# Attention with normalized queries and keys, then a spatially gated MLP: the first sixth of a hand-written instruction order laid out anew, and the last stores on two queues

## The chip, the cores and the metric

The kernel runs on one core of a Trainium2 chip. The metric is the device time of one execution, in microseconds (us). A core has a matrix engine (TensorE, PE in the profile), three other compute engines (ScalarE, ACT; VectorE, DVE; GpSimd, POOL), a synchronization engine that here only issues transfers (SyncE, SP), and 16 DMA engines that all queues share. Each engine works through its own instructions in program order; semaphores order work between engines.

## The reference

Eight batches of 12 heads, 448 positions, head size 64. The result of the attention, heads side by side (768 wide), is the input of a gated MLP.

```python
q_n, k_n = (rmsnorm(q, g_q), rmsnorm(k, g_k))      # x / sqrt(mean(x*x) + 1e-6) * g
scores = scale * np.matmul(q_n, k_n.transpose(0, 1, 3, 2))
attn = np.exp(scores - max); attn = attn / (sum(attn) + 1e-09)
x = heads side by side of np.matmul(attn, v)        # (8, 448, 768)
h = np.maximum(x @ w_in, 0.0);  u, v = two halves of h  # 512 each
v_n = (v - mean(v)) / np.sqrt(var(v) + 1e-06)
v_s = np.einsum('ts,bsd->btd', w_spatial, v_n) + b_spatial[None, :, None]
out = (u * v_s) @ w_out                             # (8, 448, 768), float32
```

## The kernel before

The 96 heads are worked in 24 groups of four, three groups to a batch. A group's q or k is a tile `raw` of 128 partitions x 896 (four heads, seven columns of 64 positions). Group 0 is loaded and normalized in two halves, so that the pipeline starts sooner. Queries and keys of the first four groups are turned by TensorE; those of later groups by transposing DMAs on SyncE's queue. The kernel leaves out the maximum before the exponential and divides at the end by sums that TensorE makes against a tile of ones.

All instructions are issued in one order, written out by hand or by a planner as the string `PLAN`; the kernel's last loop reads it word by word. A word `name.args/slots/engine` calls `op_name`; slots are buffer or PSUM bank numbers, the engine is a (ScalarE), v (VectorE), g (GpSimd) or s (SyncE). An engine thus gets its instructions in the order of the words that fall to it, and a word moved ahead or behind others on the same engine moves in that engine's queue. Buffers are reused, and an instruction also waits until its target's last reader is through: ten `raw` tiles, three of squares, 22 of exponentials, eight PSUM banks. VectorE and GpSimd operations between SBUF tiles (norms, squares) are made to take turns in the order of the plan.

The words that the text needs, with the line of the profile:

| word | what it does | engine, line |
| --- | --- | --- |
| `l.i.r`, `L.G.i` | load half r of group 0, or all of group G; i = 0 is q, 1 is k | SyncE, L309, L296 |
| `q`, `Q` / `r`, `R` | squares / their sums per row | a, v or g, L392, L394 / v, L411, L405 |
| `i`, `I` / `j`, `J` | Ln, then Exp: one over the root of the mean square | a, L428, L418 / L431, L423 |
| `n`, `N` | normalize | v or g, L446, L438 |
| `p`, `P` / `k`, `K` | transposes on TensorE / their eviction, keys times the gains | PE, L465, L457 / a or v, L373, L375, L476 |
| `T`, `Z` | transposing DMA / gains onto the turned keys | SyncE, L493 / a or v, L474, L476 |
| `S.G.u`, `E.G.u` | scores of one of the seven units of a group / their exponential | PE, L518 / a, L526 |
| `s`, `a`, `b` | one of seven passes that add up the sums, the first and the second half of attention times values | PE, L551 |
| `D`, `d`, `X` | Ln and Exp of the sums (one over the sum) / the product into the MLP's input `xt` | a, L570, L574 / v, L580 |
| `v.b.n` | load values of batch b, with a change of type | POOL's software queue, L326 |
| `wi`, `ws`, `wo` | load pieces of `w_in`, the spatial weights, `w_out`, with a change of type | POOL's software queue, L333, L337, L340 |
| `wb`, `wx` | load and copy the spatial bias | SyncE, L344 / a or v |
| `gl`, `gA`, `gB`, `gC` | load the two gains (0.5 KB each), multiply them, turn them into a column | L305, L379, L384, L387 |
| `Y.m`, `y.m` | turn the spatial weights / evict them | PE, L360 / a or v, L373, L375 |
| `V`, `U`, `W` / `c`, `u` | products with `w_in`, and the tail rows / their evictions | PE, L596, L662, L625 / a or v, L587, L589 |
| `H`, `G`, `O`, `o`, `t` | spatial product, gating, output product, eviction, store | PE L676, v L681, PE L690, a or v L373, L375, SyncE L711, L714 |
| `z.n` | n matmuls of 64 columns of the identity that nothing reads | PE, L261 |

In the plan before, 140 of these `z` matmuls stand ahead of group 0's first transposes. ScalarE's order is q.1.0, q.0.0, q.0.1, i.0, j.0, q.1.1, Q.1.1, Q.1.0, i.1, j.1, I.1, J.1 and then the first exponential, E.0.1. The spatial weights are the third transfer that GpSimd issues, and their transposes stand among the first scores.

Of the kernel before, what the change touches and what calls it, by code (L numbers as in the profile page):

```python
# [756 lines left out]
```

## Time and profile before

| | |
| --- | --- |
| runs shown | 278.58 us median (276.86 to 279.51, three runs) |
| profiled execution | 277.75 us, its span 276.0 us |
| mean granted TensorE clock | 0.979 |
| TensorE busy | 257.9 us |
| ScalarE, VectorE, GpSimd busy | 218.0, 203.2, 144.9 us |
| moved by DMA | 51.14 MB |
| first exponential starts | 16.39 us |
| last matmul ends, last store lands | 270.6 us, 274.8 us |

The profile is of one execution; times in it count from the start of the span. "Busy" is the time in which an engine had an instruction under way, and for TensorE the ends are modelled. The granted clock is the share of full speed that TensorE was given. In a line of the timeline stand start, duration, engine, line of the kernel, operation, output and input tile, and in brackets the idle time before it with what ended it. DMA shares are a mean over 16 engines and can lie a little above 1.

### The profile page before, as it was taken

The page shows a single profiled execution, that of the slowest core. Times are in us where ns is not written, and L with a number is a line of the kernel's source. Part 1 is how long each engine was busy: PE and PEld are TensorE (multiplying, and loading weights), DVE is VectorE, ACT ScalarE, POOL GpSimd, SP SyncE. Part 2 cuts the span into 40 slices and gives each one's busy share as a digit, 9 for nine tenths or more (in the row PEclk, how much of TensorE's full clock was granted, in tenths as well). Part 3 has the DMA queues.
Part 4 walks back from the last instruction along what each step waited for, and adds up shares of the span by engine and source line. Part 5 has one row for each costly group of instructions (what it writes and reads, how often), then busy time and mean ns, then how long its engine had stood idle before and what let it go on. Part 6 is the DMA issues. An engine that isn't in the chain of part 4 may idle for free.

```text
span 276.0 us, 10147 instructions
## 1 busy us (share of the span) xinstructions
PE 257.9 (93%) x4372; PEld 136.0 (49%) x4389; DVE 203.2 (74%) x355; ACT 218.0 (79%) x357; POOL 144.9 (52%) x122
## 2 busy tenths in 40 slices
PE   7479999999999999999999999999998999999992
PEld 7365555365445445444454444444553545455550
DVE  3678999888869988987985588956976184748730
ACT  3388999999989999988998989988898865330632
POOL 3073895697746798957885669654990000000000
PEclk9859999999999999999999999999999999999998
DMA  7999997999979999899799999974589400114586
GB/s 207 291 330 279 258 198 90 255 233 231 201 146 167 364 206 179 185 285 173 223 192 246 273 251 246 172 97 69 71 126 215 142 2 2 30 29 114 128 296 208
DMA packets 63073, 51.14 MB, mean 185 GB/s; under 512 B 39602, under 2 KB 58675, under 8 KB 63027
## 3 DMA queue, kind: packets, MB, share of 16 engines
q1 hardware_dynamic: 54770, 42.22, 64.2%
q0 software_dynamic: 8256, 8.27, 19.6%
q8 instruction: 34, 0.56, 0.9%
q14 instruction: 13, 0.10, 0.1%
HBM read 38.55 MB, written 11.01 MB: 180 GB/s over the span
## 4 chain that ended last, share of the span: by engine, by line
PE 31%; DMA 9%; POOL 8%; issue 4%; ACT 3%; SPq 1%; DVE 0%; ACTq 0%; POOLq 0%
PE ps L690 6%; DMA vt<-in_v_dram 6%; PE ps L676 6%; PE ps L551 6%; PE ps L596 5%; PE ps L662 4%; POOL nrm L438 4%; PE ps L518 3%; POOL sqt L394 3%; DMA qT<-nrm 3%; ACT et L526 2%; PE ps L625 2%; POOL vt L326 1%; SPq L493 1%; ACT rc L574 0%
## 5 line engine op out<-in xcount | busy, mean ns | idle before, releaser
L526 ACT ACTIVATE et<-ps 128x896 bf16<-128x896 f32 x168 | 146.0, 923 | 12.7 <-PE ps L518 11.3
L438 POOL TENSOR_TENSOR nrm<-raw,rs 128x896 bf16<-128x896 f32 x40 | 67.3, 1691 | 27.6 <-ACT rs L423 9.6
L518 PE MATMUL ps<-qT,kT 64*32 64x448 bf16 x1344 | 61.7, 358 | 3.4 <-DVE kT L476 1.1
L394 POOL TENSOR_TENSOR sqt<-raw 128x896 f32<-128x896 f32 x28 | 46.8, 1680 | 16.9 <-DVE vn L653 9.2
L551 PE MATMUL ps<-et,vt 64*32 64x448 bf16 x1344 | 52.1, 350 | 2.0 <-DMA vt<-in_v_dram 1.0
L405 DVE TENSOR_REDUCE ss<-sqt 128x14 f32<-128x896 f32 x46 | 48.4, 1075 | 4.4 <-ACT sqt L392 3.1
L662 PE MATMUL ps<-xt,w_in 128*128 128x448 bf16 x192 | 43.4, 353 | 0.2
L518 PEld LDWEIGHTS <-kT 64*32 64x32 bf16 x1344 | 22.1, 90 | 32.4 <-issue 22.5
L580 DVE TENSOR_TENSOR xt<-ps,rc 128x448 bf16<-128x448 f32 x48 | 27.9, 617 | 12.0 <-ACT rc L574 6.9
L690 PE MATMUL ps<-w_out,gt 128*128 128x384 bf16 x192 | 36.5, 326 | 0.0
L596 PE MATMUL ps<-w_in,xt 128*128 128x512 bf16 x127 | 33.9, 380 | 0.9 <-issue 0.3
L551 PEld LDWEIGHTS <-vt 64*32 64x32 bf16 x1344 | 24.6, 92 | 16.2 <-issue 3.8
L373 ACT ACTIVATE os<-ps 128x384 f32<-128x384 f32 (+1 forms) x34 | 16.4, 491 | 15.1 <-PE ps L690 14.1
L676 PE MATMUL ps<-w_spT,vn 128*128 128x448 bf16 (+1 forms) x128 | 27.7, 353 | 0.2 <-DVE xt L580 0.2
L551 PE MATMUL ps<-et,ones 64*32 64x448 bf16 x672 | 27.7, 349 | 0.0
L662 PEld LDWEIGHTS <-w_in 128*128 128x128 bf16 x192 | 17.2, 97 | 20.8 <-issue 7.4
L681 DVE TENSOR_TENSOR gt<-ps,us 128x448 bf16<-128x448 f32 x32 | 19.1, 618 | 10.4 <-PE ps L676 7.4
L690 PEld LDWEIGHTS <-gt 128*128 128x128 bf16 x192 | 18.1, 98 | 15.4 <-issue 2.7
L637 DVE BATCH_NORM_STATS2 s<-vs 128x6 f32<-128x512 bf16 (+1 forms) x32 | 21.9, 683 | 1.6 <-ACT vs L587 1.1
L326 POOL DMA_DIRECT2D vt<-in_v_dram x34 | 22.9, 679 | 0.0
L375 DVE COPY os<-ps 128x384 f32<-128x384 f32 (+1 forms) x30 | 16.5, 554 | 8.4 <-PE ps L690 6.3
L589 DVE TENSOR_SCALAR vs<-ps 128x512 bf16<-128x512 f32 (+1 forms) x24 | 16.3, 684 | 7.5 <-PE ps L596 3.5
(63 smaller groups left out, 251.2 us busy)
## 6 DMA issues: line engine op xcount, KB each, us to landing
out_dram<-os SPq DMA_DIRECT2D x55, 192.0 KB, 3.2
raw<-in_k_dram SPq DMA_DIRECT2D x23, 448.0 KB, 6.0
raw<-in_q_dram SPq DMA_DIRECT2D x23, 448.0 KB, 7.4
vt<-in_v_dram POOLq DMA_DIRECT2D x14, 224.0 KB, 7.9
vt<-in_v_dram POOLq DMA_DIRECT2D x20, 112.0 KB, 5.0
w_in<-in_moe_w_in_dram POOLq DMA_DIRECT2D x8, 192.0 KB, 12.3
w_out<-in_moe_w_out_dram POOLq DMA_DIRECT2D x1, 768.0 KB, 8.2
raw<-in_k_dram SPq DMA_DIRECT2D x2, 224.0 KB, 3.8
```

The lines of the kernel that those rows point to most:

```text
L326: pool.dma_start(out=vts[b % 2][64 * halves[0]:64 * halves[0] + 64 * len(halves), g].rearrange("p r c d -> p r (c d)"), in_=src)
L394: port(eng, eng.tensor_tensor(out=t, in0=x, in1=x, op=ALU.mult))
L405: dve.tensor_reduce(out=sss[G % 3][:, i].rearrange("p r c -> p (r c)"), in_=sqt[where.pop(("sq", G, i))].rearrange("p r (c d) -> p (r c) d ...
L438: port(eng, eng.tensor_tensor(out=nrm[sl[0]].rearrange("p c r d -> p r c d"), in0=raw[where["raw", G, i]].rearrange("p r (c d) -> p r c d" ...
L518: pe.matmul(out=ps[at:at + 32, sl[n], 0:S], lhsT=kT[64 * r:64 * r + 64, c, 64 * hh + 32 * x:64 * hh + 32 * x + 32], rhs=qT[64 * r:64 * r + ...
L526: act.activation(out=ets[sl[0]], in_=ps[:, a:b + 1:b - a, 0:S], func=AF.Exp, bias=0.0, scale=1.0)
L551: pe.matmul(out=ps[32 * l:32 * l + 32, where[kind, G][0], 0:S], lhsT=w, rhs=et_of(G, r, c)[at:at + 64], start=(n == 1), stop=(n == C), til ...
L580: dve.tensor_tensor(out=xts[b % 2][:, 2 * g + half, :], in0=ps[:, where.pop(("ab"[half], G))[0], 0:S], in1=rcs[where["rc", G]], op=ALU.mult)
L596: pe.matmul(out=ps[:, bank, :], lhsT=xts[b % 2][:, j, 128 * m:128 * m + 128], rhs=w_in[:, j % 2, j // 2, DH:], start=(n == 1 and j == 2 * ...
L662: pe.matmul(out=ps[:, bank, 0:S], lhsT=w_in[:, j % 2, j // 2, 128 * f:128 * f + 128], rhs=xts[b % 2][:, j, :], start=(n == 1 and j == 2 * ...
L676: pe.matmul(out=ps[:, sl[0], 0:S], lhsT=vns[b % SLOTS["vn"]][rows, m, 128 * f:128 * f + 128], rhs=w_spT[rows, m, :], start=(m == 0), stop= ...
L690: pe.matmul(out=ps[:, sl[0], 0:384], lhsT=gts[b % 2][:, f, 128 * m:128 * m + 128], rhs=w_out[:, f, 384 * h:384 * h + 384], start=(f == 0), ...
```

## The change

The words up to about the first third of the kernel's plan are ordered anew, and some change their engine; from about group 9 on the order is the old one, with other buffer numbers. The same words are there before and after but for the points named here.

- Group 0: `i.0` and `j.0` stand ahead of `q.0.1` on ScalarE; both norms of the first half go to GpSimd; the key gains are loaded by SyncE between the first two and the next two loads.
- The order on ScalarE at the start is q.1.0, q.0.0, i.0, j.0, q.0.1, q.1.1, i.1, j.1, Q.1.0, Q.1.1, E.0.2, k.0.1, I.1, J.1, E.0.1, E.0.0, E.0.3: all of group 0's first six units come ahead of group 1's.
- The spatial weights are loaded behind `Q.2.1` on GpSimd (group 2, the third), their transposes stand behind most of group 1's scores, and two pieces of `w_in` are issued ahead of the values `v.0.0`.
- 115 `z` matmuls stand ahead of group 0's first transposes, 25 further back.
- Group 3's and later squares, norms and evictions change engines; the values of batch 1 are loaded later.
- At the end, the second half of the last tail is evicted by VectorE instead of ScalarE, and its two stores are issued by ScalarE and SyncE instead of both by SyncE.

```diff
-setup//v l.1.0/0 gl.0//g z.1/f q.1.0/0/a l.0.0/1 z.5/f q.0.0/1/a z.11/f l.0.1 q.0.1//a z.1/f z.3/f z.11/f gl.1//g
-l.1.1 z.5/f z.1/f L.1.1/2 r.1.0//v r.0.0//v i.0//a L.1.0/3 j.0//a q.1.1//a gA//v z.1/f z.35/f r.0.1//v n.0.0//v
-Q.1.1/2/a z.34/f n.1.0//v z.9/f Q.1.0/1/a z.23/f r.1.1//v gB/2 gC//v i.1//a p.0.0/4 k.0.0/0/v p.1.0/0 k.1.0/0/v
-S.0.1/56 R.1.1//v ws//g R.1.0//v Y.2/1 y.2//v S.0.0/23 j.1//a Y.3/1 n.1.1//g v.0.1//g I.1//a J.1//a N.1.0/0/v Y.0/0
-P.1.0/4 N.1.1/1/v P.1.1/7 v.0.2//g L.2.0/4 v.1.0//g K.1.0/1/v E.0.1/0/a y.3//a E.0.0/1/a v.0.0//g n.0.1//g p.0.1/1
-y.0//a K.1.1/1/v S.1.5/45 S.1.1/23 Q.2.0/0/a R.2.0//v v.1.3//g L.2.1/5 S.1.6/67 Q.2.1/2/a wi.1.1//g E.1.5/2/a
-wi.0.1//g Y.1/0 p.1.1/5 E.1.6/3/a R.2.1//v S.1.3/67 s.1.6.0/4 y.1//v k.0.1//v I.2//a wi.0.3//g E.1.1/4/a J.2//a
-L.4.1/6 k.1.1//v E.1.3/5/a S.1.2/01 E.1.2/6/a s.1.5.0 a.1.1.0/5 S.0.3/23 s.1.3.0 N.2.1/2/v E.0.3/7/a S.1.4/67
-E.1.4/8/a L.3.0/7 a.1.6.0 L.3.1/8 s.1.1.0 S.1.0/01 a.1.5.0 P.2.1/3 N.2.0/3/v P.2.0/2 L.6.1/9 wi.1.3//g wi.1.2//g
-E.1.0/9/a Q.3.0/1/v S.0.6/67 K.2.1/2/v wi.0.0//g Q.3.1/0/g R.3.0//v s.1.2.0 b.1.1.0/3 S.0.2/01 b.1.6.0 a.1.2.0 s.1.0.0
-wb Q.4.1/2/g K.2.0/2/v b.1.4.0 E.0.6/a/a s.1.4.0 R.3.1//v wi.1.0//g S.2.2/67 E.0.2/b/a D.1/0/a L.4.0/0 a.1.0.0 a.1.4.0
-s.0.0.0/2 Q.4.0/1/v E.2.2/c/a S.0.4/01 E.0.4/d/a a.1.3.0 wi.0.2//g s.0.6.0 I.3//a s.0.1.0 b.1.0.0 L.5.1/3 d.1//a
-Q.6.1/0/v b.1.2.0 X.1.0//v S.0.5/67 J.3//a v.1.1//g S.2.1/01 s.0.3.0 N.3.0/0/g s.0.2.0 b.1.3.0 a.0.6.0/4 a.0.1.0
-b.1.5.0 E.0.5/e/a v.1.2//g X.1.1//v E.2.1/f/a S.2.0/56 E.2.0/g/a a.0.4.0 s.0.5.0 b.0.3.0/7 L.6.0/2 s.0.4.0 R.4.0//v
-S.2.4/01 b.0.0.0 b.0.2.0 a.0.3.0 E.2.4/h/a b.0.5.0 L.7.0/1 a.0.0.0 a.0.5.0 L.5.0/5 s.2.1.0/6 S.2.3/01 b.0.1.0
-Q.5.1/1/a P.3.0/5 R.4.1//v R.6.1//v N.3.1/1/g P.3.1/3 a.0.2.0 E.2.3/i/a Q.5.0/2/g S.2.6/01 K.3.0/3/v b.0.6.0 I.4//a
-s.2.4.0 K.3.1/3/v D.0/1/a J.4//a E.2.6/j/a N.4.0/2/g b.2.1.0/5 L.7.1/4 S.3.0/23 R.5.0//v b.2.0.0 s.2.2.0 E.3.0/k/a
-S.2.5/01 E.2.5/l/a R.5.1//v wx//v s.2.0.0 d.0//a T.4.0/1 s.2.3.0 b.2.6.0 b.2.2.0 s.2.6.0 X.0.0//v b.0.4.0 S.3.1/23
-E.3.1/4/a b.2.4.0 a.2.0.0/0 s.2.5.0 a.2.5.0 a.2.3.0 a.2.4.0 I.5//a a.2.1.0 N.4.1/3/g T.4.1/0 S.3.4/12 D.2/0/a J.5//a
-b.2.5.0 a.2.2.0 X.0.1//v E.3.4/3/a b.2.3.0 N.5.1/0/v T.5.1/1 S.3.3/34 N.5.0/1/g a.2.6.0 S.3.2/67 U.0.2.0/2 V.0.1.1/1
-d.2//a V.0.1.0 X.2.1//v V.0.2.1/5 X.2.0//v V.0.1.2 T.5.0/0 U.0.2.1 Q.6.0/0/a U.0.2.2 R.6.0//v Z.4/1/v V.0.2.0
-E.3.2/8/a S.4.2/67 E.3.3/9/a L.9.0/7 c.0.1//v I.6//a J.6//a N.6.1/2/g S.4.0/34 B.0.1//v u.0.2//a Z.5/0/v E.4.2/6/a
...
+setup//v z.2/f z.2/f l.1.0/0 gl.0//g q.1.0/0/a r.1.0//v l.0.0/1 q.0.0/1/a r.0.0//v i.0//a z.17/f gl.1//s l.0.1 j.0//a
+n.0.0//g q.0.1//a z.45/f z.21/f gA//v l.1.1 L.1.0/2 gB/0 gC//v q.1.1//a r.0.1//v n.1.0//g z.28/f r.1.1//v p.0.0/1
+k.0.0/0/v i.1//a j.1//a Q.1.0/2/a p.1.0/5 k.1.0/0/v S.0.2/23 n.0.1//g R.1.0//v n.1.1//g p.0.1/4 S.0.1/67 L.1.1/3
+p.1.1/5 S.0.0/01 Q.1.1/1/a R.1.1//v k.1.1//v E.0.2/0/a L.2.1/4 k.0.1//a S.0.3/23 Q.2.1/0/g I.1//a ws//g J.1//a
+N.1.1/0/v S.0.4/45 E.0.1/1/a S.0.5/67 E.0.0/2/a v.0.1//g P.1.1/1 v.0.2//g N.1.0/1/v P.1.0/0 K.1.1/1/v K.1.0/1/v
+L.2.0/5 Q.2.0/2/v R.2.0//v S.1.6/01 wi.0.1//g E.0.3/3/a wi.0.2//g v.0.0//g S.1.1/23 E.0.4/4/a E.0.5/5/a S.1.0/45
+s.0.5.0/7 s.0.1.0 s.0.4.0 E.1.6/6/a S.1.5/01 s.0.3.0 R.2.1//v E.1.1/7/a S.1.4/23 s.1.6.0/6 s.0.0.0 wi.0.3//g E.1.5/8/a
+S.1.2/01 s.0.2.0 s.1.1.0 E.1.0/9/a L.3.1/6 s.1.0.0 Q.3.1/1/g S.1.3/45 E.1.2/a/a R.3.1//v s.1.5.0 Y.2/1 Y.3/0 I.2//a
+J.2//a L.3.0/7 Q.3.0/2/g E.1.3/b/a R.3.0//v I.3//a N.2.1/2/v wi.0.0//g y.2//a Y.1/5 y.3//a S.0.6/01 Y.0/4 N.2.0/3/v
+wi.1.3//g J.3//a wi.1.1//g E.1.4/c/a P.2.1/3 P.2.0/2 E.0.6/d/a N.3.0/0/v P.3.0/1 y.0//a wi.1.2//g b.1.6.0/0 wb y.1//v
+b.1.0.0 K.2.1/2/v K.2.0/2/v s.0.6.0 L.5.1/8 s.1.4.0 wi.1.0//g S.2.6/45 L.4.1/9 S.2.0/23 L.4.0/1 b.1.4.0 K.3.0/3/v
+a.0.4.0/1 Q.4.1/0/g a.0.3.0 b.1.2.0 Q.4.0/1/a D.0/0/a a.0.2.0 a.1.1.0/7 b.1.1.0 v.1.3//g E.2.6/e/a S.2.1/45 E.2.0/f/a
+a.0.0.0 L.5.0/0 a.1.4.0 E.2.1/g/a s.1.2.0 a.0.5.0 S.2.3/23 N.3.1/1/g R.4.0//v a.1.3.0 a.1.2.0 R.4.1//v E.2.3/h/a
+S.2.2/45 a.0.6.0 a.1.0.0 a.1.6.0 P.3.1/3 s.2.1.0/2 s.1.3.0 E.2.2/i/a b.0.2.0/5 b.0.4.0 Q.5.1/2/v I.4//a s.2.6.0
+Q.5.0/1/v R.5.1//v L.9.0/3 b.1.3.0 K.3.1/3/v L.6.0/2 D.1/1/a a.0.1.0 J.4//a Q.6.0/0/g N.4.1/2/v S.2.5/34 b.0.3.0
+b.1.5.0 L.6.1/4 s.2.0.0 b.2.6.0/6 N.4.0/3/g a.1.5.0 s.2.3.0 d.1//a X.1.1//v E.2.5/j/a b.0.6.0 S.2.4/34 b.2.2.0
+R.5.0//v a.2.2.0/0 X.1.0//v T.4.1/0 T.4.0/1 d.0//a b.0.5.0 E.2.4/k/a Q.6.1/2/v s.2.5.0 a.2.0.0 a.2.6.0 I.5//a J.5//a
+N.5.1/0/g s.2.2.0 s.2.4.0 b.2.3.0 X.0.0//v N.5.0/1/g b.2.1.0 S.3.0/34 b.2.0.0 b.2.5.0 b.2.4.0 b.0.1.0 D.2/1/a d.2//a
+L.8.1/5 X.2.1//v E.3.0/l/a a.2.1.0 a.2.3.0 b.0.0.0 X.0.1//v S.3.1/12 S.3.3/67 E.3.3/7/a S.3.2/34 a.2.4.0 a.2.5.0
+X.2.0//v V.0.1.0/5 S.3.4/67 E.3.2/c/a E.3.4/a/a U.0.2.2/0 U.0.2.1 R.6.0//v Z.4/1/v U.0.2.0 u.0.2//v V.0.1.1 E.3.1/9/a
+S.4.1/34 S.4.2/67 R.6.1//v E.4.1/6/a E.4.2/b/a S.4.0/01 L.7.1/7 Q.7.1/1/v V.0.1.2 c.0.1//v I.6//a W.0/2 T.5.1/1
+S.4.4/34 c.0.3//v E.4.0/1/a Z.5/0/v S.4.5/67 J.6//a N.6.0/2/v E.4.5/4/a V.0.2.0/0 U.0.0.2/5 E.4.4/8/a T.5.0/0 S.5.1/12
+S.5.6/67 U.0.0.0 U.0.0.1 V.0.2.2 V.0.2.1 L.7.0/6 L.8.0/9 u.0.0//v S.5.0/34 E.5.1/d/a S.5.5/12 E.5.6/0/a S.3.5/56
+U.0.3.2/7 B.0.1//v U.0.3.0 U.0.3.1 Q.7.0/0/a c.0.2//a V.0.0.0/0 z.1/f V.0.0.2 E.5.0/5/a E.3.5/e/a z.1/f V.0.0.1
+L.10.1/1 S.5.4/34 S.3.6/56 R.7.0//v E.5.5/i/a z.8/f s.3.0.0/1 s.3.5.0 s.3.1.0 s.3.2.0 T.6.0/2 u.0.3//v R.7.1//v I.7//a
+E.5.4/f/a J.7//a S.5.2/23 B.0.2//v E.3.6/g/a v.1.0//g a.3.0.0/7 a.3.3.0 b.3.2.0/4 s.3.3.0 a.3.5.0 E.5.2/h/a S.4.6/56
+a.3.4.0 b.3.5.0 N.6.1/3/g T.6.1/0 B.0.3//v c.0.0//v B.0.0//v s.3.6.0 E.4.6/2/a a.3.6.0 Q.9.0/2/g s.3.4.0 wx//a D.3/0/a
+b.3.0.0 a.3.2.0 S.4.3/23 S.5.3/56 Q.8.0/0/g v.1.1//g v.1.2//g N.7.1/0/g T.7.1/1 a.3.1.0 M.0//a E.4.3/3/a s.4.6.1/01
+R.8.0//v v.2.2//g L.14.0/8 E.5.3/k/a s.4.1.1 m.0//a Z.6/2/v N.7.0/1/g s.4.2.1 s.4.5.1 b.3.1.0 S.6.1/23 E.6.1/j/a
+A.0.1//v s.4.4.1 b.3.6.0 A.0.0//v A.0.2//v s.4.0.1 A.0.3//v L.10.0/0 s.4.3.1 b.3.4.0 b.3.3.0 d.3//a X.3.1//v D.4/1/a
+S.6.4/56 Q.8.1/1/g X.3.0//v U.0.1.2/2 U.0.1.0 U.0.1.1 H.0.0/3 E.6.4/e/a R.9.0//v G.0.0//v wo//g H.0.3/4 v.2.0//g
+G.0.3//v z.3/f u.0.1//a H.0.1/0 S.6.3/56 S.6.0/34 b.4.6.1/72 b.4.4.1 b.4.0.1 d.4//a Z.7/3/a G.0.1//v D.5/0/a b.4.5.1
+b.4.2.1 R.8.1//v b.4.3.1 a.4.4.1/01 E.6.0/l/a S.6.2/34 E.6.3/c/a Q.10.0/0/g a.4.5.1 a.4.0.1 a.4.6.1 T.7.0/3 E.6.2/9/a
+d.5//a L.9.1/2 b.4.1.1 a.4.2.1 I.8//a R.10.0//v a.4.1.1 a.4.3.1 v.2.1//g S.7.0/56 z.4/f X.4.1//v Q.10.1/2/g S.7.3/34
+E.7.0/g/a X.4.0//v J.8//a z.1/f N.8.1/2/g T.8.1/0 z.1/f H.0.2/7 X.5.1//v X.5.0//v z.3/f E.7.3/a/a G.0.2//v S.7.5/56
+S.7.2/01 Q.9.1/1/v R.9.1//v S.7.4/23 E.7.5/7/a N.8.0/3/g E.7.2/8/a z.3/f T.8.0/1 E.7.4/f/a L.11.1/4 V.1.2.0/4
...
-W.8/70 o.7.1.1//a t.7.1 o.7.3.0/4/a o.7.3.1//a t.7.3
+W.8/70 o.7.1.1//a t.7.1 o.7.3.0/4/a o.7.3.1//v t.7.3//as
...
         if m == 3:
-            for at in sorted({tail_at(b, 0), tail_at(b, 1)}):
+            for n, at in enumerate(sorted({tail_at(b, 0), tail_at(b, 1)})):
                 cols = [h for h in range(2) if tail_at(b, h) == at]
                 cols = slice(384 * cols[0], 384 * cols[-1] + 384)
-                sync.dma_start(out=out_c[b][6][:, cols], in_=t[at:at + 64, cols])
+                engines[(e or "ss")[n]].dma_start(out=out_c[b][6][:, cols], in_=t[at:at + 64, cols])
             return
```

More of the change, by code (lines that the diff above doesn't have):

```diff
@@ L152 @@
+G.6.2//v V.7.1.1 V.7.1.2 W.7/035 c.7.1//v o.5.2.0/1/v B.7.0//v O.5.0.0/1 o.6.3.0/3/v U.7.3.2 o.5.0.0/0/a O.5.1.1/2
+o.6.3.1//v u.7.3//a B.7.1//v c.7.3//a O.6.2.0/3 t.6.3 o.5.1.1//a U.7.2.1 B.7.3//v t.5.1 U.7.2.2 U.7.0.2 M.7//a
+O.5.2.1/1 m.7//a t.4.0 A.7.0//v O.6.2.1/5 A.7.1//v o.5.2.1//a A.7.3//v O.5.0.1/7 A.7.2//v o.6.2.0/3/a H.7.3/0
 o.6.2.1//a u.7.0//a t.6.2 O.6.1.0/2 o.5.0.1//a G.7.3//v H.7.1/1 u.7.2//v t.5.0 o.6.1.0/4/v O.6.1.1/3 H.7.2/5 t.5.2
```

197 lines of the change are left out of this document (90 added, 107 removed).

## The prediction

> **What bounds the kernel now.** I first read the busy shares and the forty slices of the page.
>
> ```profile
> PE 257.9 (93%) x4372; PEld 136.0 (49%) x4389; DVE 203.2 (74%) x355; ACT 218.0 (79%) x357; POOL 144.9 (52%) x122
> PE   7479999999999999999999999999998999999992
> ACT  3388999999989999988998989988898865330632
> ...
> PEclk9859999999999999999999999999999999999998
> ```
>
> TensorE (PE) sets the time. The slices before 21 us are the ones with low digits, and there the granted clock falls to 0.5. The rest is in the table of busy times by stretch (columns: PE, weight loads, VectorE, ScalarE, GpSimd, then clock, DMA share, GB/s).
>
> ```profile
> 7.30:25.00 17.70, 12.58 (x158) 8.73 (x157) 12.70 (x19) 11.29 (x21) 7.58 (x11) 0.71 1.09 305
> 25.00:60.00 35.00, 33.38 (x625) 18.73 (x632) 32.04 (x46) 34.22 (x54) 26.03 (x20) 1.00 1.00 214
> 60.00:265.00 205.00, 200.82 (x3420) 100.03 (x3427) 154.55 (x280) 164.94 (x271) 108.80 (x83) 1.00 0.81 167
> 11.56:21.70 10.14, 7.33 (x88) 5.64 (x88) 6.17 (x9) 6.31 (x12) 6.52 (x10) 0.50 1.09 333
> ```
>
> From 60 us on PE is idle 4.2 us of 205, so a lead or a delay on PE at 60 us reaches the end. From 25 to 60 us ScalarE is busy 34.22 of 35 us and PE 33.38: both are full. Waste can be removed only before 25 us: 5.1 us of PE idle behind the dummies, and 10.14 us at half clock with 7.33 us of work in it, 3.7 us lost. But the DMA share there is 1.09: what runs earlier must also be loaded earlier.
>
> The timeline gives the chain of the start.
>
> ```profile
> 13.69 0.95 ACT L392 ACTIVATE sqt<-raw 128x896 f32<-128x896 f32 x1 [3.49 <-DMA raw<-in_q_dram]
> 16.39 0.92 ACT L526 ACTIVATE et<-ps 128x896 bf16<-128x896 f32 x1
> 12.90 1.26 PE L360 MATMUL ps<-ident,gt 64*64 64x64 bf16 x14 [1.70 <-DMA gt<-in_moe_w_spatial_dram]
> 16.11 1.89 PE L360 MATMUL ps<-ident,gt 64*64 64x64 bf16 x21 [1.07 <-DVE w_spT L375]
> ```
>
> PE waits for the spatial weights (12.9 us), then for their eviction. The first exponential starts at 16.39 us, behind the squares of group 1, whose q load lands at 13.6 us.
>
> **The change, part by part.** Times below are from the span's start.
>
> *Group 0.* Before, ScalarE's first `i` stands behind `q.0.1`, which waits for a load until 6.58 us. After, it stands ahead: the first sums end at about 5.2 us (3.37 plus two squares and two reductions, 0.57 and 0.6 each), `i` and `j` take 0.29 and 0.21, so GpSimd normalizes at 5.7 to 6.5 us. Its 0.95 us replaces VectorE's 0.615. PE has 115 dummies ahead (5.63 us / 140 = 0.040 each, 4.6 us) and the little `gB`, so the transposes start at 7.0 to 7.5 us, before at 8.39: **-1.0 us**. I take that with 0 and -1.4 as ends.
>
> *First exponential.* It stands behind both squares of group 1. Without the spatial weights ahead of it on the DMA (2.1 us of share between 6 and 10 us) the second of these loads lands between 9.5 us (1.2 us behind its neighbour, the spacing of the later landings) and 11.5 us (13.6 less 2.1); I take 10.3. Square 0.95, then `E.0.2` at 11.3 us, 5.1 us ahead of 16.39. In between, `k.0.1` (0.94, by the nearest ScalarE copy of 128x896, 1.04) and `I`, `J` of group 1 follow, and the 13th exponential comes at about 26.4 us, where it is at 31.1 us now. That lead is 4.7 us, but it is not PE work: by the program, PE has done 17 sums and value passes (8 s, 6 a, 3 b) before that 13th exponential now, and 10 (all s) after. Seven owed passes of 0.19 us are 1.3 us.
>
> *PE idle after the dummies.* Before, the brackets are 0.78, 1.13, 1.70, 1.07 and 0.39: 5.1 us. After, PE waits 0.4 us for the second half's norm, 1.0 us for its key eviction, 1.15 us for group 1's turned queries and keys (VectorE: a key eviction of group 0 at 14.3 to 15.0, norms 2.18, transposes at half clock 0.9, evictions 0.69 and 0.62: 19.3), and about 0.9 us for exponentials that free banks: 3.4 us.
>
> *Value loads.* This is the term that decides. The four software-queue value loads now issue from 16.05 us and land 2.5 us apart, the fourth, `v.0.0`, last:
>
> ```profile
> gt<-in_moe_w_spatial_dram POOLq DMA_DIRECT2D x1, 392.0 KB, 9.9
> vt<-in_v_dram POOLq DMA_DIRECT2D x1, 224.0 KB, 7.0
> vt<-in_v_dram POOLq DMA_DIRECT2D x1, 224.0 KB, 12.1
> ```
>
> (from issue to landing, for issues at 3.0, 16.05 and 18.5 us, so the last lands at 30.6 us). After, GpSimd squares group 2's keys first (loaded at about 11.9, 1.68 us), issues the spatial weights at 13.6 us, and on the same queue come `v.0.1`, `v.0.2`, two `w_in` pieces (1.4 us apart where they land now), then `v.0.0`. With the weights landing as fast as the first value load (7.0 us, 20.6) plus 0.9 us for their larger size, `v.0.0` lands at 21.5 + 3 x 2.5 + 2 x 1.4 = 31.8 us; with their own 9.9 us, at 33.8. The passes `a.0.*` and `b.0.*` need it, and the first of them, `a.0.4.0`, stands ahead of `S.2.1` and so of the 17th exponential. PE gets to it at 29.5 to 30.2 us: 26.4, two exponentials (0.81 each), an eviction, a square and an `Ln` (1.8 us in all). **Wait 2.1 us**, ends 0 and 4.3. So PE idle is 5.5 instead of 5.1: **+0.4 us**. Behind `a.0.4.0` on PE wait the scores of group 2, behind those ScalarE. (The transposes of the spatial weights are reached at about 23 us, between their two landings of 21.5 and 23.5: 0 to 0.5 us, within these ends.)
>
> *Clock.* Now the clock falls at 11.56 us, after a stretch with PE busy about half, and returns at 21.7, 5.6 us after dense work began at 16.11. After, work is as sparse between 8 and 19 us, dense from 19.4 us, and by that row the clock returns at 25.0 us: 13.4 us of half clock with some 9 us of work, 4.5 us lost against 3.7. **+0.8 us**, ends 0 and +1.7; the far end partly hides the wait for `v.0.0`, as PE then arrives later.
> The Trainium skill ("TensorE: Matmul & The Clock Gate", "What's actually happening") says that one busy window of about 3.4 us releases the clock, and that the window runs freely. The 5.6 us of the trace agree with that as a part of one window and a whole one. By the page the clock could be back at 22.8 us (19.4 plus 3.4); this term would then be -0.2 us and the sum 1.0 us lower.
>
> *Dummies.* 25 of the 140 move to between 50 and 80 us, where PE was idle 0.67 us in 55 to 80: 25 x 0.040 = 1.0 us, of which 0 to 0.67 is covered. **+0.7 us**.
>
> *Other engines.* Squares, norms and evictions change hands. Each engine's sum stays within 0.5 us (VectorE loses and gains 8.2 us by rows of 1.09, 0.68, 0.39), under PE. SP is passed by one 0.5 KB load (`gl.1`, 0.47 us of issue, below the DMA's own pace). The transposes of group 5 get two raw loads (1.2 us of DMA each) ahead of them on SP: now the last is issued at 47.28 and lands 3.5 us later, under scores of group 4; after, I get 50 to 51.4 us against scores wanted at 50.9: **+0.3 us**, ends 0 and 1.0. `v.1.1` and `v.1.2` move from 33 to 36 us to about 58 us, land 5 us later and are wanted from 67 us: nothing.
>
> *Tail.* Now two ScalarE evictions in a row (270.54 to 271.53), then:
>
> ```profile
> 271.81 1.19 SPq L711 DMA_DIRECT2D out_dram<-os  x2
> ```
>
> After, VectorE does the second beside the first (0.56, done at 271.1) and one store goes through ScalarE's queue. SP is busy issuing until 271.71 anyway, so the last landing comes forward by one issue at most, 0.6 us, and the data pipe is full until 274.25, which may leave 0. A store issued by ScalarE isn't in this trace; by the SP row it costs 0.6 us, unhidden. **-0.4 us**, ends -0.9 and +0.3.
>
> Sum: -1.0 + 0.4 + 0.8 + 0.7 + 0.3 - 0.4 = **+0.8 us**. The owed passes are in the PE ledger already; but the ledger took each wait alone, and PE at 25 to 60 us has no slack for 1.3 us of passes to be caught up beside exponentials. I add half, +0.7 (ends 0 and 1.3): **+1.5 us**. The profiled execution has a span of 276.0 and a time of 277.75 us, so 279.25; it lies 0.83 us under the median of the runs shown (278.58), so I predict **280.1 us** on that scale, which the rivals use too, within the 1% that measurement can tell from no change (2.8 us).
>
> **Rivals.**
> *The lead carries (faster).* If `v.0.0` lands by 30 us, ScalarE, busy 34.22 of 35 us, is what the early exponentials relieve: -4.7 + 1.3 for the passes = -3.4, dummies half hidden +0.4, tail -0.6: -3.6, or 275.0 us. For it: ScalarE's share. Against: DMA share above 1 until 40 us. Chance 0.20.
> *The value load starves PE (slower).* The spatial weights take their own 9.9 us, `v.0.0` lands at 33.8 us or later, PE waits 4 us. It decides from a wait of about 2 us: idle of 1.7 us at 11.2 to 12.9 us came with the half clock, which then cost 3.7 us over 10 us. Wait +2, half clock again +2: 284.1 us. For it: the row of 9.9 us. Against: that row is from the slow first 11 us (230 to 300 GB/s, later 380). Chance 0.27.
> *The change doesn't reach its aim.* The second load of group 1 lands at 11.5 us or later, and the first exponential with it at 12.5 us; what follows moves with the loads, by 1.2 us, instead of by the order, and meets `v.0.0` without a wait. Start -1.0, shift +1.2, dummies +0.3 (covered), tail -0.4: 278.7 us. Chance 0.08.
> My forecast has 0.45, and of that 0.08 lies above 281.4.
>
> Range: 274.5 to 284.5; beyond it I leave under 0.1 at each end. Faster by over 1%: 0.20; within: 0.45; slower: 0.35.
>
> **What would show it.** Right: first exponential at 11 to 12 us; an idle PE before a value matmul (L551) at 29 to 34 us, released by the load of `vt`; clock at 0.5 beyond 21.7 us; the last store under 274.8. Wrong: no such wait, and at 60 us PE ahead of before; or a half clock that never comes; or a transpose landing after 52 us that holds the scores of group 5.

## The result, and the profile after

The changed kernel takes **294.57 us** (median of four runs, 293.12 to 297.42) against 277.72 us (275.71 to 279.51) before: a ratio of 1.062, 95% interval 1.052 to 1.072. Forecast were 280.1 us and a range up to 284.5. The profiled execution after took 297.42 us, its span 295.6. One fact is needed for all that follows: executions of the changed kernel fall into two groups. Of ten in all, seven took 293 to 298 us and three 288.1 to 289.4 us, so 10.4 to 11.7 us of the loss are there in every execution and some 7 us more come and go.

The page after, with TensorE's (PE) and ScalarE's (ACT) slices and the granted clock:

```profile
PE 267.3 (90%) x4389; PEld 136.5 (46%) x4389; DVE 204.2 (69%) x354; ACT 220.2 (74%) x357; POOL 144.6 (49%) x122
...
PE   7489899678999999999999859999999799999990
...
ACT  5489599659977999989999918898889666420540
PEclk9959799899999999999999968999999999999997
```

The start has gained digits, but the clock now falls in four places ahead of the end instead of one, and PE has holes at the eighth to ninth slice and the 23rd to 24th. The table of busy times by stretch (PE, weight loads, VectorE, ScalarE, GpSimd, clock, DMA share, GB/s):

```profile
7.30:25.00 17.70, 12.12 (x186) 6.57 (x185) 12.60 (x16) 12.86 (x19) 12.08 (x14) 0.81 1.07 309
25.00:60.00 35.00, 31.74 (x512) 17.41 (x505) 27.36 (x36) 28.42 (x47) 17.57 (x16) 0.90 0.98 193
...
15.26:22.30 7.04, 6.16 (x78) 3.49 (x82) 5.67 (x8) 6.21 (x10) 5.77 (x9) 0.52 1.11 275
56.20:59.60 3.40, 3.40 (x31) 0.96 (x29) 2.49 (x4) 3.10 (x5) 1.92 (x3) 0.54 1.13 340
172.00:179.80 7.80, 6.12 (x144) 2.94 (x152) 1.34 (x2) 1.96 (x4) 1.76 (x2) 0.56 1.06 318
```

From 25 to 60 us ScalarE was busy 34.22 of 35 us before, and is 28.42 now. PE's own timeline names what ended its longest waits:

```profile
34.47 0.94 PE L551 MATMUL ps<-et,vt 64*32 64x448 bf16 x16 [0.81 <-DMA vt<-in_v_dram]
...
55.30 0.57 PE L518 MATMUL ps<-qT,kT 64*32 64x448 bf16 x16 [2.10 <-DMA qT<-nrm]
...
66.17 0.38 PE L518 MATMUL ps<-qT,kT 64*32 64x448 bf16 x6 [1.81 <-ACT et L526]
...
173.68 1.32 PE L551 MATMUL ps<-et,vt 64*32 64x448 bf16 x24 [4.47 <-DMA vt<-in_v_dram]
```

The first is `v.0.0`, which the prediction feared; the others are `T.5.0` (turned queries of group 5), an exponential of group 5, and the values `v.4.3`. Where the time went shows best at fixed points of the order. `M.b` is the first Ln of the MLP's norm of batch b (L643); r1 to r3 are three more profiled executions of the same changed kernel, from the lower group (us from the start of the span):

| execution | time | 1st exp | 13th | 29th | 37th | M.0 | M.1 | M.3 | M.4 | M.7 | end |
| --- | --- | --- | --- | --- | --- | --- | --- | --- | --- | --- | --- |
| before | 277.75 | 16.39 | 31.13 | 50.57 | 57.33 | 61.07 | 88.40 | 146.26 | 176.90 | 258.31 | 276.0 |
| after | 297.42 | 13.43 | 27.67 | 50.81 | 65.22 | 70.30 | 98.99 | 156.51 | 193.65 | 276.10 | 295.6 |
| r1 | 288.54 | 10.92 | 25.37 | 48.21 | 60.95 | 67.30 | 96.07 | 154.38 | 186.31 | 267.35 | 286.7 |
| r2 | 289.42 | 11.19 | 25.55 | 47.43 | 59.45 | 64.53 | 93.97 | 153.12 | 187.18 | 268.35 | 287.6 |
| r3 | 288.14 | 11.11 | 25.47 | 47.77 | 62.57 | 67.65 | 96.54 | 155.30 | 185.75 | 266.87 | 286.3 |

Up to the 29th exponential the changed order is level (after) or 2.4 to 3.1 us ahead (r1 to r3). At M.0 it is 9.2 us behind (3.5 to 6.6 in r1 to r3), by M.1 1.4 to 2.1 us more; then, in this execution, 6.5 us between M.3 and M.4 (1.3, 3.4 and -0.2 in r1 to r3), and 1.6 to 1.8 us between M.7 and the end.

### The profile page after: what moved, and what is told of

Its sections match the earlier page's. It is cut to its first block, busy times and chain, and to the rows that moved or that the text cites. A ratio compares the mean times of both kernels' runs of the same rounds, so it can differ in the third digit from the quotient of the medians.

```text
span 295.6 us, 10156 instructions
## 1 busy us (share of the span) xinstructions
PE 267.3 (90%) x4389; PEld 136.5 (46%) x4389; DVE 204.2 (69%) x354; ACT 220.2 (74%) x357; POOL 144.6 (49%) x122
## 4 chain that ended last, share of the span: by engine, by line
PE 58%; DMA 17%; ACT 9%; POOL 4%; issue 4%; DVE 3%; SPq 2%; DVEq 0%; POOLq 0%; ACTq 0%
PE ps L551 12%; PE ps L662 9%; DMA vt<-in_v_dram 9%; PE ps L596 9%; PE ps L518 9%; PE ps L690 8%; PE ps L676 7%; ACT et L526 5%; DMA qT<-nrm 5%; DMA raw<-in_k_dram 3%; POOL nrm L438 3%; PE ps L625 3%; DVE ss L405 1%; SPq L493 1%; ACT sqt L392 1%
## 5 line engine op out<-in xcount | busy, mean ns | idle before, releaser
L438 POOL TENSOR_TENSOR nrm<-raw,rs 128x896 bf16<-128x896 f32 x38 | 64.0, 1693 | 45.7 <-ACT rs L423 14.4
L518 PE MATMUL ps<-qT,kT 64*32 64x448 bf16 x1344 | 63.9, 368 | 11.9 <-DVE kT L476 4.5
L394 POOL TENSOR_TENSOR sqt<-raw 128x896 f32<-128x896 f32 x29 | 48.5, 1680 | 23.9 <-DVE vn L653 9.5
L551 PE MATMUL ps<-et,vt 64*32 64x448 bf16 x1344 | 50.4, 360 | 5.9 <-DMA vt<-in_v_dram 5.3
L596 PE MATMUL ps<-w_in,xt 128*128 128x512 bf16 x144 | 37.0, 387 | 0.0
L551 PEld LDWEIGHTS <-vt 64*32 64x32 bf16 x1344 | 23.0, 95 | 21.6 <-DMA vt<-in_v_dram 6.5
L375 DVE COPY os<-ps 128x384 f32<-128x384 f32 (+1 forms) x31 | 17.1, 555 | 11.0 <-PE ps L690 6.4
L570 ACT ACTIVATE rc<-ps 128x448 f32<-128x448 f32 x24 | 12.5, 545 | 12.4 <-PE ps L551 12.2
```

The costliest lines, as they stand in the source:

```text
L394: port(eng, eng.tensor_tensor(out=t, in0=x, in1=x, op=ALU.mult))
L438: port(eng, eng.tensor_tensor(out=nrm[sl[0]].rearrange("p c r d -> p r c d"), in0=raw[where["raw", G, i]].rearrange("p r (c d) -> p r c d" ...
L518: pe.matmul(out=ps[at:at + 32, sl[n], 0:S], lhsT=kT[64 * r:64 * r + 64, c, 64 * hh + 32 * x:64 * hh + 32 * x + 32], rhs=qT[64 * r:64 * r + ...
L551: pe.matmul(out=ps[32 * l:32 * l + 32, where[kind, G][0], 0:S], lhsT=w, rhs=et_of(G, r, c)[at:at + 64], start=(n == 1), stop=(n == C), til ...
L596: pe.matmul(out=ps[:, bank, :], lhsT=xts[b % 2][:, j, 128 * m:128 * m + 128], rhs=w_in[:, j % 2, j // 2, DH:], start=(n == 1 and j == 2 * ...
```

## The experiments

The first four ran on one chip, where the kernel before had a median of 276.94 us; r1 and e5 to e7 shared another (277.70), e8 to e10 a third (278.92), and e11 ran on the first again (278.36); r2 and r3 ran on a fourth. In e1 to e4 line numbers are two or three lower, since their plan has fewer lines.

**Theory 1** (dummies): `u.0.3` on VectorE evicts a PSUM bank that the eight dummies `z.8/f` write too (64 other columns of it), and so waits for them; behind it stands the sum `R.7.1`, behind that on ScalarE `I.7`, and behind that the exponential E.5.4. VectorE's and ScalarE's timelines after:

```profile
63.34 0.62 DVE L589 TENSOR_SCALAR us<-ps 128x448 bf16<-128x448 f32 x1 [3.91 <-PE ps L261]
63.88 1.08 DVE L405 TENSOR_REDUCE ss<-sqt 128x14 f32<-128x896 f32 x1
...
65.00 0.32 ACT L418 ACTIVATE ls<-ss,eps 128x28 f32<-128x28 f32 x1 [3.31 <-DVE ss L405]
65.22 0.90 ACT L526 ACTIVATE et<-ps 128x896 bf16<-128x896 f32 x1
```

Exponentials stood still from 61.7 to 65.2 us. The rival, **theory 2**: two loads, `L.8.1` and `L.7.1`, stand ahead of `T.5.0` on SyncE's queue, and a third, the values `v.1.0`, is issued by GpSimd 0.6 us ahead of it; they make it late. A third place is the load `v.4.3`.

*e1: another bank for the dummies.*

```diff
-V.0.0.0/0 z.1/f V.0.0.2 E.5.0/5/a E.3.5/e/a z.1/f V.0.0.1 ... E.5.5/i/a z.8/f
+V.0.0.0/0 V.0.0.2 E.5.0/5/a E.3.5/e/a V.0.0.1 ... E.5.5/i/a z.8/9
```

> The changed kernel, but the ten identity matmuls that stand between V.0.0.0 and s.3.0.0 no longer write the PSUM bank of U.0.3: two are dropped, eight write bank 1, which s.3.0.0 takes right after them. Theory (the identity matmuls share bank 7 with U.0.3, so the eviction u.0.3 on VectorE, and behind it the sums R.7.1 and ScalarE's I.7, wait for them): u.0.3 starts at about 61.2 us instead of 63.3, ScalarE's idle time before I.7 falls from 3.3 to about 1.1 us, the time falls by 2 to 3.4 us. Rival (the order of loads alone is to blame, the dummies are innocent): u.0.3 still starts near 63.3 us and the time changes by less than 1 us. Second rival (the next late thing takes over): u.0.3 is early, but the time falls by less than 1 us.

*e2: none of the 25 later dummies.*

```diff
-z.1/f ... z.1/f ... z.8/f ... z.3/f ... z.4/f ... z.1/f ... z.1/f ... z.3/f ... z.3/f
```

> The changed kernel without the 25 identity matmuls that stand behind the first scores; their output is read by nothing. Theory: as in the run with the other bank, and 25 x 0.03 us of TensorE on top: 3 to 4.5 us faster than the changed kernel. Rival (they do keep the clock up): the granted clock falls to 0.5 somewhere between 55 and 85 us where it is full in the changed kernel, and the time falls by less than 1 us or grows.

*e3: the loads ahead.*

```diff
-L.6.1/4 ... L.8.1/5 X.2.1//v ... L.7.1/7 Q.7.1/1/v ... E.3.6/g/a v.1.0//g
+L.6.1/4 L.7.1/7 L.8.1/5 ... X.2.1//v ... Q.7.1/1/v ... E.3.6/g/a
-v.1.3//g
+v.1.3//g v.1.0//g
```

> The changed kernel, but the raw loads L.7.1 and L.8.1 are issued ahead of the transposes T.4.1 and T.4.0, right behind L.6.1, and the values v.1.0 right behind v.1.3, so that they move between 30 and 41 us, where the DMA share fell to 0.44. Theory (T.5.0 lands late, at 55.2 us, because these three share the DMA with it): T.5.0 lands by 52.5 us, TensorE waits under 0.5 us for it instead of 2.1, the clock stays full from 56 to 60 us, and the time falls by 3 to 4.5 us. Rival (the transposes themselves are late because their norms are): T.5.0 is issued and lands as late as before, the time changes by less than 1 us.

*e4: v.4.3 ahead.*

```diff
-v.4.2//g ... E.15.4/l/a v.4.3//g u.3.0//v
+v.4.2//g v.4.3//g ... E.15.4/l/a u.3.0//v
```

> The changed kernel, but the values v.4.3 are issued right behind v.4.2, at about 147 us instead of 162. Theory (the wait of 4.5 us at 169 us and the half clock behind it come from this one load): no wait over 0.5 us for values between 160 and 180 us, clock full there, 4 to 6.5 us faster where the wait was, less in the median if only some executions have it. Rival (a later value load takes its place, because the DMA is full): a wait for values of 2 us or more stays between 160 and 185 us and the time changes by less than 1.5 us.

Measured: e1 287.25 us (ratio to before 1.036, 1.031 to 1.041), e2 287.08 (1.040, 1.032 to 1.049), e3 286.23 (1.032, 1.027 to 1.037), e4 287.73 (1.036, 1.029 to 1.043). All four came out alike, about 7 us under the 294.57 of the changed kernel, and no profile of them shows the wait for `v.4.3`, also where its load was not touched (all the same one execution of e4 took 295.8 us, and one each of e2 and e3 290.7 and 291.6). So the medians tell nothing apart; the traces do. From the arrival of `T.5.0` to M.0 it is 15.0, 14.7 and 14.9 us in after, r1 and r3, and 15.0 in e4, each with one window of half clock in it (13.5 in r2, with none); in e1 and e2, with one window too, it is 12.9. `u.0.3` is no longer released by the dummies there, and the wait of 1.81 us is gone. **Theory 1 is worth 2.0 us.** That the dummies keep the clock up, the rival of e2, does not show: without them the clock is full from 57.4 to 279.2 us. But in e1 and e2 PE waits 2.95 and 3.08 us for `T.5.0`, so M.0 stays at 66.7. In e3 it is the other way round: the transposing DMA lands in 2.9 us instead of 7.7 (r3), PE does not wait for it, and the wait for E.5.4 stays at 1.81 us. What the trace says of that one DMA (`T.5.0`, L493; L491 in e3) and its time to landing, r3 first, then e3:

```profile
L493 SPq DMA_TRANSPOSE qT<-nrm x1: 2313/2313/2313, 45.0 to 45.0; - x1
...
DMA to landing us min/median/max: 7.7/7.7/7.7
```

```profile
L491 SPq DMA_TRANSPOSE qT<-nrm x1: 1220/1220/1220, 45.5 to 45.5; - x1
...
DMA to landing us min/median/max: 2.9/2.9/2.9
```

Ahead of it in r3 SyncE issued the two loads and `T.5.1`, and GpSimd the values `v.1.0`:

```profile
42.37 1.24 SPq L296 DMA_DIRECT2D raw<-in_k_dram  x2
43.71 1.23 SPq L493 DMA_TRANSPOSE kr<-nrm  x1
45.05 2.31 SPq L493 DMA_TRANSPOSE qT<-nrm  x1
...
44.45 0.76 POOL L326 DMA_DIRECT2D vt<-in_v_dram  x1
```

Between the issue of `T.5.0` and its landing the packets of `v.1.0` took 27% of the DMA engines' time in r3 (2.1 of 7.7 us) and 21% in after (1.5 of 7.2 us). e3 moved all three loads at once, so it shows their price together; what each costs alone no run separates.

Each loss was mended alone, and the other was still there. Next, the control and both mends together.

*r1: the changed kernel again.*

> The changed kernel unaltered, on the chip and beside the runs of the kernel before that the next kernels share. Its timed runs gave 293.1 to 297.4 us, while four kernels that differ from it by a few words gave 285.1 to 291.6 with one of 295.8. In its profile 16.7 us were lost after 146 us to two things that the four do not show: the wait of 4.47 us for the values `v.4.3` at 173.7 us and the 8 us of half clock behind it. Theory A (a collision of loads that comes and goes with small differences in time): the repeat can come out without it, at 286 to 289 us, with M.4 behind M.3 by 30 to 31 us instead of 37.1. Theory B (it belongs to this order as it stands, and each of the four edits happened to remove it): 293 to 297 us again and the same wait. In both, the first 62 us and the tail are as in the profile: T.5.0 late by 2 to 3 us, 1.8 us of TensorE idle before S.5.2, and the last store issued 3.4 us behind its eviction.

One execution took 288.54 us, the others 295.99 to 297.67. Theory A holds as far as that: the same order comes out with and without 8 us.

*e5: e2 and e3 together.*

> Both edits together: none of the 25 later dummies (as in e2_no_late_z) and the loads of groups 7 and 8 and the values v.1.0 as in e3_loads_ahead. If the two losses are separate causes, their gains add: T.5.0's wait goes (2 to 3 us and some 2 us of half clock) and so does the wait of u.0.3 (some 3 us of ScalarE), so the first Ln of the MLP's norm (M.0), at 66.8 and 65.0 us in the two alone, comes at 62 to 63.5 us (before 61.1), no TensorE idle over 1 us lies between 45 and 70 us, and the time is 282 to 284.5 us. If they stand in for one another (PE behind, or ScalarE full, whichever is mended), M.0 stays at 65 us or later and the time at 286 to 287. The start and the tail are left as the change has them, which should hold 1.5 to 2.4 us of the rest in the tail alone.

**281.73 us** (ratio 1.016, 1.011 to 1.021), all four executions between 281.2 and 283.5. M.0 comes at 61.67 us: theories 1 and 2 (with all three loads) add up, and together they are most of the loss up to M.0. One wait of 3.23 us for `v.0.0` is left at 30.7 us, which does not move M.0.

*e6: R.7.1 ahead of u.0.3.*

```diff
-u.0.3//v R.7.1//v I.7//a
+R.7.1//v u.0.3//v I.7//a
```

> The changed order with u.0.3 and R.7.1 exchanged on VectorE, dummies and their bank left alone. If the dummies cost through the queue on VectorE (u.0.3 waits for the eight dummies in its bank, R.7.1 behind it, I.7 on ScalarE behind R.7.1, and E.5.4 behind I.7), then I.7 comes without 3.3 us of idle ScalarE, the 1.8 us of TensorE idle before S.5.2 are gone, and the kernel is 1.5 to 3 us under the repeat of the changed one, like e1_z8_other_bank. If the dummies cost by their own time on TensorE (25 x 0.040 = 1.0 us) or by the bank alone, the exchange gives nothing: within 0.5 us of the repeat.

Executions of 284.17 and of 292.57 to 294.32 us: two groups as in r1, each 3.4 to 4.4 us lower. Its ScalarE and VectorE:

```profile
59.83 2.54 ACT L526 ACTIVATE et<-ps 128x896 bf16<-128x896 f32 x3
62.24 0.33 ACT L418 ACTIVATE ls<-ss,eps 128x28 f32<-128x28 f32 x1
...
59.08 2.08 DVE L405 TENSOR_REDUCE ss<-sqt 128x14 f32<-128x896 f32 x2
64.08 0.62 DVE L589 TENSOR_SCALAR us<-ps 128x448 bf16<-128x448 f32 x1 [2.92 <-PE ps L261]
```

`u.0.3` still waits for the dummies, and nobody is behind it: `I.7` follows without a gap. From the arrival of `T.5.0` to M.0 it is 12.9 us again. The price was the queue on VectorE, not the dummies' time. The profiled execution (294.32 us) has no wait for `v.4.3`; it has 2.22 us for `v.0.0`, 3.22 for `T.5.0`, 2.26 without a named releaser at 84.6 us and 2.35 for a transposing DMA at 227 us, each with 1.7 us of half clock behind it.

*e7: before, with the new tail.*

```diff
-o.7.3.1//a t.7.3
+o.7.3.1//v t.7.3//as
```

(with the two changed lines of `op_t`.)

> The kernel before with only the change's tail: the second half of the last tail evicted by VectorE, its two stores issued by ScalarE and SyncE. My prediction had -0.4 us for it. The traces of the changed kernels show SyncE's store waiting for the landing of ScalarE's (issued 3.3 to 3.5 us behind its eviction; waits of SyncE on out_dram 2.7 to 3.7 us). If that wait is the tail's price, the last store is issued at about 274.4 us instead of 271.8, and the span is 1.5 to 2 us longer than before's: 277.8 us against 276.0, ratio 1.005 to 1.007. If the late issue hides under stores that are still under way: within 0.5 us of before. By the prediction: 0.4 us under it.

279.65 us, ratio 1.0053 (1.0003 to 1.0103); from M.7 to the end 19.7 us instead of 17.7. The timelines of ScalarE, VectorE and SyncE at the end of after, then SyncE's waits there, and the store and the wait of e7:

```profile
288.34 0.48 ACT L373 ACTIVATE os<-ps 64x384 f32<-64x384 f32 x1 [0.28 <-PE ps L625]
288.86 0.56 ACTq L711 DMA_DIRECT2D out_dram<-os  x1
...
288.43 0.56 DVE L375 COPY os<-ps 64x384 f32<-64x384 f32 x1 [0.95 <-PE ps L625]
...
292.47 0.47 SPq L711 DMA_DIRECT2D out_dram<-os  x1
```

```profile
SPq L711 <- DMA out_dram<-os: 3.2, 1, 3.2
```

```profile
273.85 0.47 SPq L711 DMA_DIRECT2D out_dram<-os  x1
```

```profile
SPq L711 <- DMA out_dram<-os: 3.0, 1, 3.0
```

VectorE's half is ready at 288.99 us and SyncE's queue free at 289.23, but the store is issued at 292.47: it waits for the landing of the other store into the same block of the output (at 292.40), though the two write different columns of it.

*e8: before, second eviction on VectorE, both stores on SyncE* (`t.7.3//ss`).

> The kernel before with only the eviction of the last tail's second half on VectorE; both stores stay on SyncE's queue. With the stores of the change on two queues SyncE's waited for the landing of ScalarE's (e7_before_new_tail: ratio 1.005, from its last MLP norm M.7 to the end of the span 19.7 us against 17.7). If that wait is the whole price of the change's tail, it is gone here: 17.2 to 17.7 us from M.7 to the end, and the time is 0 to 0.6 us under before's. If the eviction on VectorE costs by itself, some of the 2 us stays.

278.23 us, ratio 0.9997 (0.9964 to 1.0030), no wait of that kind, 17.5 us from M.7 to the end. The wait was the whole price, and the eviction on VectorE gains nothing that can be measured.

*e9: e5 with both stores on SyncE.*

> e5_no_late_z_loads_ahead (281.7 us) with the stores of the last tail both on SyncE's queue. The tail is worth 2 us by itself, so 279.5 to 280 us if it adds to the others; the rest over before's 277.7 is then the wait for the values v.0.0 (3.2 us at 30.7 us) less what the early exponentials bring.

280.60 us (279.5 to 280 were expected), ten executions of 279.17 to 287.88, ratio 1.0063 (1.0017 to 1.0109); in its profile the span is 277.4 us, M.0 62.1, M.7 259.7.

*e10: e9 with v.0.0 ahead.*

```diff
-wi.0.1//g E.0.3/3/a wi.0.2//g v.0.0//g S.1.1/23
+v.0.0//g wi.0.1//g E.0.3/3/a wi.0.2//g S.1.1/23
```

> The same with one more edit: the load of the values v.0.0 is issued ahead of the two pieces of w_in instead of behind them, which lands it 2.4 to 2.8 us earlier, at about 28 us. If the early exponentials are a lead that this wait alone takes away, TensorE's idle time of 3.2 us before the first pass over v.0.0 shrinks to under 1 us, the seventeenth to thirty-third exponentials come 2 us earlier than in e9, and the time is 277 to 278 us: level with before or under it. If ScalarE or the loads of groups 2 to 4 hold the pace there, another wait takes its place and the time stays within 0.7 us of e9's.

280.28 us, ratio 1.0048 (1.0008 to 1.0088), 0.0015 from e9. The expectation missed its point, as e9's own profile has no wait for `v.0.0` either: that wait is 0 to 3.2 us from execution to execution. What e10 does tell is the worth of the lead. Its 29th exponential starts at 47.62 us, 2.95 ahead of before, the 33rd 2.7 ahead, the 37th 1.5, the 41st 0.1, and M.0 stands at 60.96 against 61.07. No wait over 0.6 us lies in between; ScalarE is simply full (busy 13.49 of 13.60 us) in the stretch that follows the 29th:

```profile
47.60:61.20 13.60, 12.72 (x214) 5.70 (x220) 11.00 (x20) 13.49 (x22) 9.74 (x8) 1.00 0.73 164
```

Before M.0 both orders have the same 40 exponentials; the changed one puts them ahead of squares, evictions and a copy of 1.03 us (`wx`) that ScalarE then still has to do. Up to M.0 ScalarE is busy 51.7 us in e10 and 49.7 before, with the same exponentials in it; `wx`, which stood on VectorE before, is 1.0 of these 2.0 us. The lead is spent on that and on work put off; it is not a gain.

*e11: e9 with the 25 dummies, and the exchange of e6.*

> The changed order with all 25 later dummies kept, and three mends: the loads as in e3_loads_ahead, u.0.3 behind R.7.1 on VectorE as in e6_r71_ahead, and both stores of the last tail on SyncE's queue. It differs from e9_e5_tail_one_queue (280.6 us, ratio 1.0063 to before) by the dummies and the exchange alone. If the dummies cost TensorE their own time, as the prediction priced them (25 x 0.040 = 1.0 us, 0.7 unhidden), the ratio is 1.009 to 1.010, 281.4 us or more; if they lie in idle time or beside the exponentials, 280.3 to 280.9 us like e9. If the two modes of the changed kernel (288.5 and 296 us) came from these dummies, some runs lie 8 us above the rest; if they came from the wait for T.5.0 and the half clock behind it, none do.

285.93 us, five executions of 281.94 to 286.05 and one of 293.14; ratio 1.0224 (1.0146 to 1.0301). That is 1.6% over e9, more than the dummies' own 1.0 us. In its profile M.0 is 1.4 us later than in e9 (after 5.1 us more at half clock), M.1 another 0.9; the rest is a wait of 3.37 us for a transposing DMA at 219 us with two windows of half clock behind it. From M.0 to M.1 stand 15 of the dummies: it is 27.65 to 27.66 us in the four kernels without them (e2, e5, e9, e10; before 27.33) and 28.55 to 29.44 in the executions with them that I profiled outside e6. A row of them shows 0.19 us each when they stand alone, and one waits 0.5 us for VectorE. So these 15 cost **0.9 to 1.8 us**. One of the six executions lies 7 us or more above the rest, in a kernel whose profile has `T.5.0` on time; e9, without dummies, has two of ten at 285.0 and 287.9 us. So neither the dummies nor the wait for `T.5.0` can be all of what comes and goes.

*r2, r3: two more profiles of the changed kernel.*

> The changed kernel unaltered, one more profiled execution. Two theories of the 8 us by which most of its executions (293 to 298 us) lie above its best (288.5 us). A, one cause: the wait for the values v.4.3 (4.47 us in the profile of 297.4 us, 1.82 us in that of 288.5 us) with two windows of half clock behind it (3.4 us); then every profile above 293 us has it, at about 170 us from the start. B, several: each long wait for a load or a transposing DMA (2 us or more) is followed by 1.7 or 3.4 us lost at half clock, and which of them is long differs from execution to execution; then a profile above 293 us shows two or three such waits, in other places too (the scores of group 5 at 53 to 57 us, the value pass over v.0.0 at 30 us, scores at 213 to 230 us).

> The same once more. A: a wait for v.4.3 of over 4 us in every profile above 293 us. B: other waits of 2 us or more, each with 1.7 to 3.4 us of half clock behind it.

Both came from the lower group (289.42 and 288.14 us), so an execution above 293 us was not caught again. Against A speak e6 (above, 294.32 us without any wait for `v.4.3`) and the range of that wait: 4.47 us in after, 1.82 in r1, 2.42 in r2, none in r3. PE's timelines of r2 and r1:

```profile
168.25 1.03 PE L551 MATMUL ps<-et,vt 64*32 64x448 bf16 x24 [2.42 <-DMA vt<-in_v_dram]
```

```profile
168.90 0.76 PE L551 MATMUL ps<-et,vt 64*32 64x448 bf16 x24 [1.82 <-DMA vt<-in_v_dram]
```

**What stays open**: why these late landings come together more often in the changed order (and in e6) than in e1 to e5, which differ from it by a few words. The chip is a rival that was not tested: e1 to e4 ran on one chip and r1 on another, and for the first four executions of the changed kernel the chip is not on record. Against it speaks that on the chip of r1, where three of four executions were in the upper group, e5 had none in four. No version tried beats the kernel before; e8 is level with it.

## Why the prediction was wrong, step by step

The sum was +1.5 us, of which nothing after 61 us but the dummies and the tail. In r1 to r3 the end is 10.3 to 11.6 us later than before. Of that 3.5 to 6.6 us stand at M.0 already, 1.4 to 2.1 come by M.1, 0.4 to 4.5 by M.7 and 1.6 to 1.8 behind it. The mended runs price the parts: `T.5.0` with its half clock 4.6 to 5.8 us (M.0 at 66.7 to 66.8 in e1 and e2 against 61.0 to 62.1 in e5, e9 and e10), `u.0.3` 2.0, the dummies between M.0 and M.1 0.9 to 1.8, the tail 1.6 to 2.0: 9.1 to 11.6. That this sum comes so near is partly chance. `T.5.0` landed at 53.9 us in e1 and e2 and at 51.1 to 52.7 in r1 to r3, so it costs less there; r2 has lost only 3.5 us at M.0 and loses 3.4 more at `v.4.3`.

- *Group 0, first exponential, lead.* Right in the main. Group 0's transposes start at 7.17 us (forecast 7.0 to 7.5), the first exponential at 13.43 us, later than forecast, and at 10.9 to 11.2 in r1 to r3 (forecast 11.3; 11 to 12); the 13th at 27.67 and 25.4 to 25.6 (26.4). That the lead is not work gained for the end was the right reading, and e10 shows it: the rival of 275.0 us falls.
- *Value loads.* "The term that decides" did not. Forecast 2.1 us with ends 0 and 4.3; measured 0.81 in after, 0 to 1.45 in r1 to r3, 3.23 in e5. The mechanism is there and within its ends, but e5 and e10 reach M.0 within 0.7 us of each other with a wait of 3.2 us and with none. (Before, `v.0.0` was issued at 18.26 us and landed at 30.34, 0.3 us ahead of what the prediction read; that changes nothing.)
- *Clock at the start.* Half clock was forecast up to 25.0 us with 4.5 us lost. It lasts from 15.5 to 22.3 us, and one more window follows at 29.2 to 32.6, behind the transposes of the spatial weights. By the prediction's count, half of the busy time in it, that is 3.1 + 1.7 = 4.8 us against 3.7 before, so +1.1 for a forecast of +0.8; but r2 and r3 lack the second window, and there it is -0.7 (3.0 us). What the start loses is also not seen at M.0: e5, e9 and e10 have none, two windows and one before M.0, and reach it at 61.7, 62.1 and 61.0 us. The estimate from the Trainium skill's window ("TensorE: Matmul & The Clock Gate", "What's actually happening") had the clock back at 22.8 us, and 22.3 lies nearer to that than to my 25.0 by the row. It is no test of either, as both counted from dense work at 19.4 us and it began at 15.43. **Where I failed is that I charged half clock to the start alone.** Behind the wait for `T.5.0` and the one for `v.4.3` stand one and two windows more, 1.7 and 3.4 us (mean clocks 0.54 over 3.40 us and 0.56 over 7.80 us, stretches that hold a little full clock too), so a wait of 2 us can cost nearly 4.
- *Transposes of group 5.* The failing term: "+0.3 us, ends 0 and 1.0". Measured are waits of 2.10 us in after and 1.74 to 2.61 in r1 to r3, in after and r3 with a window of half clock behind them, and issuing the three loads earlier is worth 4.6 to 5.8 us at M.0 (e1 and e2 against e5, e9 and e10). The forecast let the transpose land 3.5 us after its issue, as before, at 50 to 51.4 us. It was issued at 48.09 us in after, hardly later than that implies, but took 7.2 us (6.8 to 7.7 in r1 to r3) and landed at 55.3; the prediction had named a landing past 52 us as its sign of being wrong. So the time from issue to landing is what was mis-sized. Two raw loads ahead of it were in the forecast, with 1.2 us of DMA each. The third load was not: the values `v.1.0` moved from 17.54 us before to 0.6 us ahead of `T.5.0`. With all three gone from there the transpose lands in 2.9 us (e3, e5, e9 to e11).
- *Dummies.* "+0.7 us" priced their time on TensorE, 25 x 0.040. Missed was who else uses the bank: eight of them write the bank that `u.0.3` reads, and VectorE's queue carries the wait to ScalarE (e1, e2, e6). That is the question of what stands behind a waiting instruction, which I did not ask, because I saw dummies as work and not as writers. Those later, between M.0 and M.1, cost 0.9 to 1.8 us where I had at most 0.6.
- *Tail.* "-0.4 us, ends -0.9 and +0.3" became +1.6 to +2.0 in the traces. I priced the issue on ScalarE's queue, and missed the wait that two queues bring: in one queue the two stores follow each other, in two SyncE's waits for the other's landing, 3.2 us.
- *From group 9 on.* "The order is the old one", costed at nothing. From M.3 to M.7 it takes 112.05 us before, 111.57 to 115.23 in r1 to r3 and 119.59 in after: the order itself costs nothing, late landings and the half clock behind them cost 7.5 us in after. The prediction had no term for them. In the one profile of the changed kernel from the upper group they and the later M.0 (70.30 us) are its distance to r1 to r3; a second such profile is lacking.
- *The rivals.* The nearest by time, 284.1 us, was right that a late transfer starves TensorE and that half clock follows from a wait of about 2 us, and wrong about the transfer.
